# A decode kernel bound by its loads: the last query tile of four weights loads goes to the upper 64 partitions by GpSimd's queue

## The chip, the cores and the metric

The kernel runs on one core of one Trainium2 chip. The metric is device time in microseconds, the median of several executions. TensorE (PE), VectorE (DVE), ScalarE (ACT), GpSimd (POOL) and SyncE (SP) run side by side, and 16 DMA engines move data between HBM and SBUF for all of them. A transfer is issued by SyncE, ScalarE or GpSimd, each through a queue of its own. SBUF has 128 partitions.

## The reference

Two layers of attention with a cached K and V (one new token, batch 2, 32 query heads over 8 K/V heads, 32,768 cached positions, head size 128), each followed by a token-mixing MLP. All values are float32.

```python
def _A_ref(x, k_cache, v_cache, wq, wo):
    q = (lambda x, *d: x.transpose(*d))((x @ wq).reshape(B, Sq, Hq, Dh), 0, 2, 1, 3)
    k = jnp.repeat(k_cache, rep, axis=1)
    v = jnp.repeat(v_cache, rep, axis=1)
    scores = jnp.einsum("bhqd,bhkd->bhqk", q, k) * (Dh ** -0.5)
    p = _softmax(scores, axis=-1)
    o = jnp.einsum("bhqk,bhkd->bhqd", p, v)
    return (lambda x, *d: x.transpose(*d))(o, 0, 2, 1, 3).reshape(B, Sq, Hq * Dh) @ wo
...
x = x + _A_ref(_layernorm(x, axis=-1), A_k_cache, A_v_cache, A_wq, A_wo)
x = x + _B_ref(_layernorm(x, axis=-1), B_w1, B_b1, B_w2, B_b2)
x = x + _A_ref(_layernorm(x, axis=-1), A_k_cache, A_v_cache, A_wq, A_wo)
x = x + _B_ref(_layernorm(x, axis=-1), B_w1, B_b1, B_w2, B_b2)
```

K and V of all heads and both batch entries are 537 MB, and each layer reads them once.

## The kernel before

The work is cut into units: one K/V head of one batch entry in one layer, 32 units in all. A unit reads K in eight chunks of 4,096 positions and then V in eight chunks. A chunk is 128 partitions by 16 KB, 2 MB. TensorE multiplies the query of the unit with the K chunks (`k_chunk`, line 426, tile `scores`), VectorE takes the maximum and transposes, ScalarE makes the exponentials (line 466), TensorE multiplies them with the V chunks (`v_chunk`, line 581, tile `acc`), and the output projection of the unit is added to a row in PSUM (`add_row`, line 246). V of a unit runs interleaved with K of the next.

Nearly the whole of SBUF is one tile, `mem`, in cells of one chunk. Cells 0 to 8 are the ring for K and V, cells 9 to 12 (`WCELL0` and on) hold weights, and a rest of five 512-word pieces follows. Cell 8 also serves as `spot()`, a turning supply of eight 512-word scratch tiles for query rows and hidden tiles.

The order of everything is written out at build time. A list `stream` holds all K and V loads in order; the loop at the end goes through it, issues each load from SyncE's queue (`load`, line 139) and the matmuls of its chunks, and counts time in chunks. Other steps are hung on that clock by `at(time, step)`: for instance the query of a unit is made about six chunks before its K begins (`make_q`, `q_products`, line 340), and the weights come ten chunks before.

Weights (`load_weights`, line 118) come for two heads at a time: four query tiles and four output tiles of 128 rows by 2 KB for each head, so 32 KB in each of 128 partitions, 4 MB, in one load from SyncE's queue. There are four pairs of heads; one pair stays for both layers, so there are seven such loads. The query of a unit is the sum of four matmuls with `xnT`, the normalised input in columns, one for each query tile.

GpSimd makes constants at the start and the powers of the layer norms (lines 271, 685, 871); it issues no transfer.

Of the kernel before, what the change touches and what calls it, by code (L numbers as in the profile page):

```python
# [13 lines left out]
P = 128  # L14
CK = 4096
# [5 lines left out]
RING = 3  # L21
# [9 lines left out]
KEPT_Q = 4  # L31
RESIDENT = (5, 7)
TWO_HEADS = ((0, 1), (2, 3), (4, 6), RESIDENT)
FOLLOWS = {2: (2.2, -0.9, -0.8, -0.7, 3.5, -0.6, -0.5, -0.4), 5: (3.05, 0.1, 0.2, 0.3, 5.1, 3.1, 3.2, 3.3)}
PIECES = (32, 16, 8, 4, 4)
THIN = 16
QT = 4
# [7 lines left out]
def gqa_mixer_kernel(ctx: ExitStack, tc: tile.TileContext, x, kt, v, wqo, cols, out):  # L45
# [17 lines left out]
    nc = tc.nc  # L63
    B, D = out.shape
# [4 lines left out]
    R = wqo.shape[2] // (4 * D)  # L69
    DT = D // P  # L70
    FT = (cols.shape[1] - 1) // 4
# [13 lines left out]

    NP = 28 + 32 * 2
    widths = dict(x=B * DT, xn=B * DT, q=KEPT_Q * R, cols=4 * FT + 1, ident=P, one=1, half=1, selg=R * QT)
    widths |= dict(selh=R, mask=QT, others=B, oz=2 * R * B, qpads=NP, unit=2 * 16, ln=16 + 2 * FT)
    small_sb = const.tile([P, sum(widths.values())], F32, name="small_sb")
    sm, w0 = {}, 0  # L90
    for name, w in widths.items():
# [6 lines left out]
    W = wqo.shape[2] // 4  # L98
    assert CK == 2 * W
    WCELL0, WCELLS = RING * RING, 4  # L100
    heads = list(range(HKV))
    passing = [h for h in heads if h not in RESIDENT]
    home = {}
    mem = const.tile([P, (WCELL0 + WCELLS) * CK + REST * QT * DH], F32, name="mem")

    def cells(k, m=1):
        return mem[:, k * CK : (k + m) * CK]

    def wq_at(h):
        return cells(home[h])[:, :W].rearrange("p (t c) -> p t c", t=DT)  # L110

    def wo_at(h):
        return cells(home[h])[:, W:].rearrange("p (t c) -> p t c", t=R)

    def load_weights(k, cell):
        for j in range(2):
            home[TWO_HEADS[k][j]] = cell + j
        nc.sync.dma_start(cells(cell, 2), wqo[k])


    busy = [0] * 2 * (WCELL0 + WCELLS + 1)
# [73 lines left out]
    ident = sm["ident"]  # L195
# [59 lines left out]
    def first_input():  # L255

        t = spot()
        cen, sq = (t[:, k * B * DT : (k + 1) * B * DT].rearrange("p (b d) -> p b d", b=B) for k in range(2))
        m, rs = (t[:, (2 * DT + k) * B : (2 * DT + k + 1) * B] for k in range(2))
        p = misc()  # L260
        nc.tensor.matmul(p[:, : B * DT], ones, xcols.rearrange("p b d -> p (b d)"), start=True, stop=True)
        nc.vector.tensor_reduce(m, p[:, : B * DT].rearrange("p (b d) -> p b d", b=B), axis=AX.X, op=ALU.add)
        nc.vector.tensor_scalar_mul(m, m, 1.0 / D)
        for b in range(B):
            nc.vector.tensor_scalar_sub(cen[:, b, :], xcols[:, b, :], m[:, b : b + 1])
        nc.vector.tensor_mul(sq, cen, cen)
# [27 lines left out]
    xnT = sm["xn"].rearrange("p (d b) -> p d b", b=B)  # L294
# [5 lines left out]
    spots = [0]  # L300

    def spot():

        spots[0] += 1
        return cells(RING * RING - 1)[:, spots[0] % (CK // D) * D :][:, :D]

    def to_columns(key):

# [12 lines left out]
    def unit_of(n):  # L321

        return units[n]

    q_ps, q_row, q_kept = {}, {}, {}
    kept_q = [0]

    def partner(n):

        layer, b, h = unit_of(n)  # L330
        return units.index((layer, B - 1, h)) if b == 0 and (layer == 0 or h in passing) else None

    def q_products(n, *ds):

        layer, b, h = unit_of(n)
        m = 1 if partner(n) is None else B
        for d in ds:
            if d == 0:
                q_ps[n] = bcast if N1 < n <= N3 + 2 else kept[0]
            nc.tensor.matmul(  # L340
                q_ps[n][:m, :],
                xnT[:, d, b : b + m],
                wq_at(h)[:, d, :],
                start=(d == 0),
                stop=(d == DT - 1),
            )

    def make_q(n, step, place=None):

# [339 lines left out]
    ln = sm["ln"]  # L689
# [238 lines left out]
    kbeg, k_done, vbeg, v_done, vend_of, v_from, v_to, brings, starts, t = {}, {}, {}, {}, {}, {}, {}, [], [], 0  # L928
# [13 lines left out]
    def at(time, f, *a, rank=1):  # L942
        done.setdefault(time, []).append((rank, f, a))

    HC = NCH // HALVES
    opens = {two[0]: k for k, two in enumerate(TWO_HEADS)}
    mixed = {}
    for n in range(NU):
        layer, b, h = unit_of(n)
# [19 lines left out]
                assert max(v_done[n - 2, c] for c in range(HC)) <= q2  # L969
        if n and h in opens and (units[n] == (0, 0, h) or h in passing and units[n] == (1, 0, h)):  # L970
            at(kbeg[n] - (7 if n == N3 + 2 else 10), load_weights, opens[h], WCELL0 + opens[h] % 2 * 2)
        if n in (N1 + 1, N2 + 1):
            at(kend - 0.5, turn_scores, n, 0, rank=2)
            at(kend, q_products, n + 1, 0)
            at(kend, max_1, n)
            at(kend, q_products, n + 1, 1)
            at(kend, max_2, n)
            at(kend, exponentials_at_once, n, 0)
            at(kend, q_products, n + 1, 2, 3)
            t1 = kend + 2  # L980
            assert mixed[units[n - 1][:2]] == kend == kbeg[n + 1] - 2
            at(t1, turn_scores, n, 1, rank=2)
            at(t1, exponentials_at_once, n, 1, rank=2)
            at(t1 + 1, sums, n)
            assert t1 + 1 < v_done[n, HC] - 1
        else:
            t1 = max(kend + 2, ahead + (2 if urgent else 4))
            e = kend if N1 < n <= N3 else kend + 2
            at(max(kend, e - 1), max_1, n)
            at(e, max_2, n)  # L990
            t0 = max(k_done[n, HC - 1], *(v_done[n - 1, c] for c in range(HC) if n), 0)
            if n in (N2, N3):
                t0 = max(t0, kbeg[n + 1] - 3)
            at(t0, turn_scores, n, 0)
            at(e, exponentials, n, 0)
            if n == NU - 1:
                t1 = ahead
                assert t1 >= kend + 2 and vbeg[n] == ahead
            at(t1, turn_scores, n, 1)
            at(t1, exponentials, n, 1)  # L1000
# [74 lines left out]
    t = 0  # L1075
# [11 lines left out]
    assert not done, sorted(done)  # L1087


def _layout(A_x, A_k_cache, A_v_cache, A_wq, A_wo, B_w1, B_b1, B_w2, B_b2):  # L1090

    import numpy as np

    B, HKV, SK, DH = A_k_cache.shape
    D = A_x.shape[-1]
    n = SK // CK


    keys = np.arange(SK).reshape(n, CK)
    for c0, m in GROUPS:  # L1100
        keys[c0 : c0 + m] = keys[c0 : c0 + m].reshape(P, m, CK // P).transpose(1, 0, 2).reshape(m, CK)
    k = keys.reshape(n // PACK, PACK // 2, 2, NG, 32, JT // QT, QT // SUB, SUB)
# [11 lines left out]
    return {  # L1114
        "x": np.ascontiguousarray(A_x.reshape(B * (D // P), P).T),
        "kt": kt,
        "v": A_v_cache.reshape(B * HKV, SK * DH),
        "wqo": np.stack([np.concatenate([wqo[h] for h in two], axis=1) for two in TWO_HEADS]),
        "cols": np.concatenate(cols, axis=1),
    }  # L1120

# [24 lines left out]
```

## Time and profile before

| what | value |
|---|---|
| time, median of 3 (lowest to highest) | 2491.02 us (2490.99 to 2491.31) |
| the profiled execution: its own time, its span | 2490.09 us, 2488.0 us |
| moved by DMA | 1062.51 MB, mean 427 GB/s |
| TensorE, VectorE, ScalarE, GpSimd busy | 55%, 10%, 8%, 0% |
| mean granted TensorE clock | 0.772 |

Busy shares are over the whole span. A row of a stretch gives the length, then busy time and number of instructions of each engine, the granted clock, the busy share of the 16 DMA engines (counted where a packet starts) and GB/s. A row of a DMA queue gives packets, MB and the time that its packets took as a share of 16 engines over the stretch.

### The profile page before, as it was taken

The page shows a single profiled execution, that of the slowest core. Times are in us where ns is not written, and L with a number is a line of the kernel's source. Part 1 is how long each engine was busy: PE and PEld are TensorE (multiplying, and loading weights), DVE is VectorE, ACT ScalarE, POOL GpSimd, SP SyncE. Part 2 cuts the span into 40 slices and gives each one's busy share as a digit, 9 for nine tenths or more (in the row PEclk, how much of TensorE's full clock was granted, in tenths as well). Part 3 has the DMA queues.
Part 4 walks back from the last instruction along what each step waited for, and adds up shares of the span by engine and source line. Part 5 has one row for each costly group of instructions (what it writes and reads, how often), then busy time and mean ns, then how long its engine had stood idle before and what let it go on. Part 6 is the DMA issues. An engine that isn't in the chain of part 4 may idle for free.

```text
span 2488.0 us, 20543 instructions
## 1 busy us (share of the span) xinstructions
PE 1371.4 (55%) x9302; PEld 376.2 (15%) x9302; DVE 244.9 (10%) x643; ACT 187.7 (8%) x554; POOL 4.9 (0%) x17
## 2 busy tenths in 40 slices
PE   4544445544545454657677665455455465455546
PEld 1111111111111111111121121111111111111112
DVE  1000000000000000003113110000000000010002
ACT  0000000000000000002012000000000000011002
POOL 0000000000000000000000000000000000000000
PEclk8777767876777777778888887777678677777878
DMA  9999999999999999999999999999999999999996
GB/s 421 437 432 428 433 436 430 434 435 427 436 436 432 426 436 431 427 431 407 433 427 417 428 432 432 438 430 431 432 428 438 428 429 435 431 434 431 432 431 291
DMA packets 30336, 1062.51 MB, mean 427 GB/s; under 512 B 3621, under 2 KB 3625, under 8 KB 4266
## 3 DMA queue, kind: packets, MB, share of 16 engines
q1 hardware_dynamic: 29960, 1061.17, 99.1%
q8 instruction: 73, 1.20, 0.2%
q14 instruction: 13, 0.11, 0.0%
q10 hardware_dynamic: 290, 0.04, 0.0%
HBM read 1061.19 MB, written 0.00 MB: 427 GB/s over the span
## 4 chain that ended last, share of the span: by engine, by line
DMA 73%; PE 25%; DVE 1%; issue 0%; another core or an unknown queue 0%; ACT 0%; SPq 0%; POOL 0%; ACTq 0%
DMA mem<-in_v_dram 64%; PE acc L581 20%; DMA mem<-in_kt_dram 9%; PE scores L426 3%; PE small L612 0%; PE small L455 0%; PE small L449 0%; PE bcast L340 0%; ACT S L466 0%; PE small L642 0%; PE kept L246 0%; PE kept L792 0%; PE bcast L672 0%; DVE S L551 0%
## 5 line engine op out<-in xcount | busy, mean ns | idle before, releaser
L426 PE MATMUL scores<-mem,small_sb 128*32 128x512 f32 x4096 | 631.7, 736 | 605.4 <-DMA mem<-in_kt_dram 605.2
L581 PE MATMUL acc<-mem,S 128*16 128x512 f32 x4088 | 596.8, 723 | 457.1 <-DMA mem<-in_v_dram 447.7
L426 PEld LDWEIGHTS scores<-mem,small_sb 128*32 128x32 f32 x4096 | 150.0, 129 | 988.7 <-issue 903.7
L466 ACT ACTIVATE S<-S,small_sb 128x128 f32<-128x128 f32 x240 | 123.4, 517 | 2107.9 <-DVE small_sb L457 1556.9
L581 PEld LDWEIGHTS acc<-mem,S 128*16 128x16 f32 x4088 | 132.6, 109 | 810.8 <-issue 664.4
L441 DVE TENSOR_REDUCE small_sb<-scores 128x1 f32<-128x512 f32 x64 | 44.2, 691 | 819.5 <-PE scores L426 819.5
L461 DVE STREAM_TRANSPOSE S<-scores 128x512 f32<-128x512 f32 x64 | 45.5, 710 | 116.0 <-PE acc L581 116.0
L340 PE MATMUL kept<-mem,small_sb 128*2 128x512 f32 x104 | 51.1, 617 | 1.7 <-DVE small_sb L274 1.7
L466 ACT ACTIVATION_READ_ACCUMULATOR S<-S,small_sb 128x1 f32 x240 | 44.7, 186 | 0.0
L246 PE MATMUL kept<-mem,small_sb 128*1 128x512 f32 (+1 forms) x236 | 42.4, 598 | 2.6 <-ACT mem L835 2.4
L451 DVE TENSOR_REDUCE small_sb<-small 1x4 f32<-1x128 f32 x32 | 8.9, 279 | 277.7 <-PE small L449 277.7
L614 DVE RECIPROCAL small_sb<-small 128x4 f32<-128x4 f32 x32 | 5.9, 185 | 304.6 <-PE small L612 304.6
L623 DVE TENSOR_TENSOR small_sb<-small,small_sb 128x4 f32<-128x4 f32 x31 | 5.1, 164 | 295.8 <-PE small L621 295.8
L551 DVE SCALAR_TENSOR_TENSOR S<-acc,small_sb,S 128x128 f32<-128x128 f32 x93 | 32.6, 351 | 3.3
L835 ACT ACTIVATE S<-bcast,small_sb 128x512 f32<-128x512 f32 x28 | 21.5, 777 | 87.2 <-DVE small_sb L704 85.1
L366 PE MATMUL small<-small_sb,mem 2*128 2x2 f32 x112 | 15.5, 256 | 17.9 <-DVE mem L362 17.9
L549 DVE TENSOR_SCALAR S<-acc,small_sb 128x128 f32<-128x128 f32 x31 | 10.8, 350 | 147.3 <-PE acc L581 147.3
L621 PEld LDWEIGHTS small<-small_sb,S 128*128 128x128 f32 x62 | 12.7, 258 | 48.8 <-issue 41.2
L340 PE MATMUL bcast<-mem,small_sb 128*1 128x512 f32 (+1 forms) x40 | 19.4, 600 | 0.0
L366 PEld LDWEIGHTS small<-small_sb,mem 2*128 2x128 f32 x112 | 14.3, 196 | 30.5 <-DVE mem L362 27.3
L852 DVE SCALAR_TENSOR_TENSOR acc<-S,small_sb,acc 128x512 f32<-128x512 f32 x24 | 18.1, 755 | 2.5
L449 PE MATMUL small<-small_sb 128*1 128x128 f32 x64 | 16.6, 353 | 3.1 <-DVE small_sb L447 3.1
(147 smaller groups left out, 285.3 us busy)
## 6 DMA issues: line engine op xcount, KB each, us to landing
mem<-in_kt_dram SPq DMA_DIRECT2D x14, 4096.0 KB, 22.5
mem<-in_v_dram SPq DMA_DIRECT2D x11, 4096.0 KB, 29.2
mem<-in_wqo_dram SPq DMA_DIRECT2D x7, 4096.0 KB, 37.6
mem<-in_v_dram SPq DMA_DIRECT2D x13, 2048.0 KB, 21.3
mem<-in_kt_dram SPq DMA_DIRECT2D x12, 2048.0 KB, 19.3
mem<-in_kt_dram SPq DMA_DIRECT2D x24, 1024.0 KB, 8.8
mem<-in_v_dram SPq DMA_DIRECT2D x21, 1024.0 KB, 8.8
mem<-in_kt_dram SPq DMA_DIRECT2D x2, 6144.0 KB, 24.2
```

Source lines behind the costliest of these rows:

```text
L246: nc.tensor.matmul((rows if to is None else to)[32 * g : 32 * g + b + 1, :], weights if b else weights[:, 1:], row, start=to is not None, ...
L340: nc.tensor.matmul(q_ps[n][:m, :], xnT[:, d, b : b + m], wq_at(h)[:, d, :], start=(d == 0), stop=(d == DT - 1),)
L366: nc.tensor.matmul(pt[:, r * m : (r + 1) * m], q_row[n][:m, r * DH : (r + 1) * DH], ident[:m, :m], start=True, stop=True,)
L426: nc.tensor.matmul(sc_ps[n, half][32 * g : 32 * g + 32, :], q, kc[k * NG + g], start=(i == 0 and k == 0), stop=(i == PACK - 1 and k == SUB ...
L441: nc.vector.tensor_reduce(mx[n][:, half : half + 1], sc_ps[n, half], axis=AX.X, op=ALU.max)
L449: nc.tensor.matmul(pm[:1, :P], mxa, ident, start=True, stop=True)
L461: nc.vector.transpose(S[half], sc_ps[n, half])
L466: nc.scalar.activation(s[:, :, h], s[:, :, h], AF.Exp, bias=neg[n][:, h : h + 1], scale=SCALE, accum_out=lsum[n][:, half, h : h + 1],)
L551: nc.vector.scalar_tensor_tensor(t, acc[:, k * DH : (k + 1) * DH], mask[:, k : k + 1], t, op0=ALU.mult, op1=ALU.add)
L581: nc.tensor.matmul(acc[32 * g : 32 * g + R * QT, :], S[half][:, col : col + R * QT], vc[q], start=(c == v_from[n] and q < NG), stop=(c == ...
L835: nc.scalar.activation(hid[key, f], px[key], AF.Gelu_apprx_tanh, bias=shift[key][:, f : f + 1], scale=slope[key][:, f : f + 1],)
L852: nc.vector.scalar_tensor_tensor(h if f == FT - 1 else acc, h, w, acc, op0=ALU.mult, op1=ALU.add)
```

## The change

In the loads of two pairs of heads (`UPPER`, heads 2, 3 and 4, 6), once in each layer, the last of the four query tiles of each head is left out of the load from SyncE's queue, which so becomes 28 KB in each partition. The two tiles left out go as four half tiles, 64 rows each, to partitions 64 to 127, where the two halves of a tile lie side by side: in the rest of `mem` for one pair, in the upper half of cell 8 for the other (`raise_tiles`). They go by eight loads of eight rows, every fourth partition, from GpSimd's queue, 18 chunks ahead of the weights load. Ahead of each of the eight stands a load of two words to each of eight partitions of a small tile, `step`, which nothing reads. The product with the last query tile becomes two matmuls over 64 partitions each; for this the last column block of `xnT` is also copied, its lower half to partitions 64 to 127 (`raise_input`). `spot()` turns among four tiles instead of eight. The weights of those pairs are laid out to fit.

```diff
+UPPER = (1, 2)
...
     def load_weights(k, cell):
+        tiles = 2 * (DT + R - (k in UPPER))
         for j in range(2):
-            home[TWO_HEADS[k][j]] = cell + j
-        nc.sync.dma_start(cells(cell, 2), wqo[k])
+            home[TWO_HEADS[k][j]] = cell * CK + j * (tiles // 2) * D
+        of = wqo[k].rearrange("p c -> (p c)")[: P * tiles * D].rearrange("(p c) -> p c", p=P)
+        nc.sync.dma_start(mem[:, cell * CK :][:, : tiles * D], of)
+
+    lift = {UPPER[0]: 0, UPPER[1]: 1}
+    steps = [0]
+
+    def raise_tiles(k):
+        lift[k] = 1 - lift[k]
+        w0 = (WCELL0 + WCELLS) * CK if lift[k] else (WCELL0 - 1) * CK + CK // 2
+        for j in range(2):
+            raised[TWO_HEADS[k][j]] = [mem[H:, w0 + (2 * i + j) * D :][:, :D] for i in range(2)]
+        of = wqo[k].rearrange("p c -> (p c)")[-H * 4 * D :].rearrange("(i u c) -> u i c", i=2, u=H)
+        to = mem[H:, w0 : w0 + 4 * D].rearrange("u (i c) -> u i c", i=2)
+        nc.vector.memset(sm["step"], 0.0)
+        for r in range(8):
+            u = r % 4 + H // 2 * (r // 4)
+            i = steps[0] % 16
+            steps[0] += 1
+            nc.gpsimd.dma_start(sm["step"][i::16, ::2], cols[i::16, :3:2])
+            nc.gpsimd.dma_start(to[u : u + 29 : 4], of[u : u + 29 : 4])
+
+    def raise_input():
+        p = misc()
+        nc.tensor.matmul(p[H:, :B], ident[:, :H], xnT[:, DT - 1, :], start=True, stop=True)
+        nc.vector.tensor_copy(sm["up"][H:, :], p[H:, :B])
...
-        return cells(RING * RING - 1)[:, spots[0] % (CK // D) * D :][:, :D]
+        return cells(RING * RING - 1)[:, spots[0] % (CK // D // 2) * D :][:, :D]
...
+            last = d == DT - 1
+            pairs = [(xnT[:, d, b : b + m], wq_at(h, d))] if not (last and h in raised) else [
+                (x[H:, b : b + m], t) for x, t in zip((xnT[:, d, :], sm["up"]), raised[h])
+            ]
+            for i, (x, t) in enumerate(pairs):
+                nc.tensor.matmul(
+                    q_ps[n][:m, :], x, t, start=(d == 0), stop=(last and i == len(pairs) - 1)
+                )
...
             at(kbeg[n] - (7 if n == N3 + 2 else 10), load_weights, opens[h], WCELL0 + opens[h] % 2 * 2)
+            if opens[h] in UPPER:
+                at(kbeg[n] - 28, raise_tiles, opens[h])
+                if opens[h] == UPPER[0]:
+                    at(kbeg[n] - 28, raise_input)
```

GpSimd's instructions after the start-up, before the change: a constant for the padded queries, the power of the first layer norm, then those of the mixers.

```order
L218 MEMSET small_sb 128x16
L220 MEMSET small_sb 128x92
L271 TENSOR_TENSOR mem<-mem,small_sb 128x2
L685 TENSOR_TENSOR small_sb<-small_sb 128x1
L871 TENSOR_TENSOR small_sb<-small_sb 128x1
```

The same place now; `small_sb<-in_cols_dram` is a tiny load, `mem<-in_wqo_dram` one of the eight-row loads:

```order
L251 MEMSET small_sb 128x16
L253 MEMSET small_sb 128x92
L304 TENSOR_TENSOR mem<-mem,small_sb 128x2
L144 DMA small_sb<-in_cols_dram 8x2x1
L145 DMA mem<-in_wqo_dram 8x2x1024
```

The last two rows come 16 times in a row here, in two groups of eight, and 16 times again in layer 1, after the powers of the layer changes.

TensorE at the query of the fifth unit (head 2, first layer), before; `kept_85` is the PSUM tile of the query products:

```order
L426 MATMUL scores<-mem,small_sb 32x512 x15
L340 MATMUL kept_85<-mem,small_sb 2x512 [waits DMAHW7_49]
L340 MATMUL kept_85<-mem,small_sb 2x512
L426 MATMUL scores<-mem,small_sb 32x512 x8
L340 MATMUL kept_85<-mem,small_sb 2x512 x2
```

And now; the names with SW are semaphores of GpSimd's transfers:

```order
L378 MATMUL kept_85<-mem,small_sb 2x512 [waits DMAHW7_49]
L378 MATMUL kept_85<-mem,small_sb 2x512
L460 MATMUL scores<-mem,small_sb 32x512 x8
L378 MATMUL kept_85<-mem,small_sb 2x512
L378 MATMUL kept_85<-mem,small_sb 2x512 [waits DMASW5_49,DMASW7_49,DMASW3_49,DMASW1_49]
L378 MATMUL kept_85<-mem,small_sb 2x512
L460 MATMUL scores<-mem,small_sb 32x512 x8
```

The fourth product has become two, and the first of them waits for the raised tiles. SyncE's list of loads has the same order and number, four of them with 7,168 words in a partition instead of 8,192.

More of the change, by code (lines that the diff above doesn't have):

```diff
@@ L87, in gqa_mixer_kernel @@
     widths = dict(x=B * DT, xn=B * DT, q=KEPT_Q * R, cols=4 * FT + 1, ident=P, one=1, half=1, selg=R * QT)
-    widths |= dict(selh=R, mask=QT, others=B, oz=2 * R * B, qpads=NP, unit=2 * 16, ln=16 + 2 * FT)
+    widths |= dict(selh=R, mask=QT, others=B, oz=2 * R * B, qpads=NP, unit=2 * 16, ln=16 + 2 * FT, step=3, up=B)
     small_sb = const.tile([P, sum(widths.values())], F32, name="small_sb")
@@ L107, in cells, with wq_at @@
         return mem[:, k * CK : (k + m) * CK]
-    def wq_at(h):
-        return cells(home[h])[:, :W].rearrange("p (t c) -> p t c", t=DT)
+    H = P // 2
+    raised = {}
+    def wq_at(h, d):
+        return mem[:, home[h] + d * D :][:, :D]
     def wo_at(h):
-        return cells(home[h])[:, W:].rearrange("p (t c) -> p t c", t=R)
+        w = home[h] + (DT - (h in raised)) * D
+        return mem[:, w : w + W].rearrange("p (t c) -> p t c", t=R)
     def load_weights(k, cell):
+        tiles = 2 * (DT + R - (k in UPPER))
         for j in range(2):
-            home[TWO_HEADS[k][j]] = cell + j
-        nc.sync.dma_start(cells(cell, 2), wqo[k])
+            home[TWO_HEADS[k][j]] = cell * CK + j * (tiles // 2) * D
[21 more added lines that the diff above has]
+        nc.vector.tensor_copy(sm["up"][H:, :], p[H:, :B])
     busy = [0] * 2 * (WCELL0 + WCELLS + 1)
@@ L339, in q_products @@
                 q_ps[n] = bcast if N1 < n <= N3 + 2 else kept[0]
[L340 to L346, printed above, removed]
+            last = d == DT - 1
[6 more added lines that the diff above has]
+                )
     def make_q(n, step, place=None):
@@ L1087, in gqa_mixer_kernel, with _two_heads @@
     assert not done, sorted(done)
+def _two_heads(two, parted, d):
+    import numpy as np
+    if not parted:
+        return np.concatenate(two, axis=1)
+    c = np.arange((d // P - 1) * d, d // P * d)
+    main = np.concatenate([np.delete(a, c, axis=1) for a in two], axis=1)
+    top = [np.concatenate([a[u : u + P // 2, c] for a in two], axis=1) for u in (P // 2, 0)]
+    return np.concatenate([a.ravel() for a in (main, *top)]).reshape(P, -1)
 def _layout(A_x, A_k_cache, A_v_cache, A_wq, A_wo, B_w1, B_b1, B_w2, B_b2):
@@ L1117, in _layout @@
         "v": A_v_cache.reshape(B * HKV, SK * DH),
-        "wqo": np.stack([np.concatenate([wqo[h] for h in two], axis=1) for two in TWO_HEADS]),
+        "wqo": np.stack([_two_heads([wqo[h] for h in two], k in UPPER, D) for k, two in enumerate(TWO_HEADS)]),
         "cols": np.concatenate(cols, axis=1),
```

## The prediction

> **What bounds the kernel now.** I read the page first, then stretches of the span, then SyncE's issues, and last single packets of the DMA engines. On the page:
>
> ```profile
> span 2488.0 us, 20543 instructions
> PE 1371.4 (55%) x9302; PEld 376.2 (15%) x9302; DVE 244.9 (10%) x643; ACT 187.7 (8%) x554; POOL 4.9 (0%) x17
> DMA  9999999999999999999999999999999999999996
> q1 hardware_dynamic: 29960, 1061.17, 99.1%
> q8 instruction: 73, 1.20, 0.2%
> DMA 73%; PE 25%; DVE 1%; issue 0%; another core or an unknown queue 0%; ACT 0%; SPq 0%; POOL 0%; ACTq 0%
> ```
>
> TensorE is busy for 55% of the span, while SyncE's queue q1 keeps all 16 DMA engines busy for 99.1% of it and the chain that ended last is DMA for 73%. The waits say the same: the scores matmuls stand idle until a K chunk lands. And SyncE issues a load well before the engines are free for it (rows of its timeline; the landing row is that of the seven weights loads):
>
> ```profile
> PE scores L426 <- DMA mem<-in_kt_dram: 605.2, 82, 20.3
> 218.40 0.33 SPq L139 DMA_DIRECT2D mem<-in_v_dram  x1
> 218.77 0.43 SPq L118 DMA_DIRECT2D mem<-in_wqo_dram  x1
> 237.31 0.33 SPq L139 DMA_DIRECT2D mem<-in_kt_dram  x1
> DMA to landing us min/median/max: 12.3/37.6/37.8
> ```
>
> The weights issued at 218.77 take the median 37.6 us to land, and the next K load is issued 19 us after them, so there is always work queued. What counts is therefore not the mean of the 16 engines but the engine that is last. Here are stretches of the span: a long one inside layer 0, the first change of layer, and the last microseconds of the loads. The last two numbers of a row are the busy share of the 16 engines and GB/s.
>
> ```profile
> 240.00:560.00 320.00, 162.82 (x1120) 44.49 (x1120) 22.45 (x64) 16.32 (x61) 0.00 (x0) 0.75 1.00 433
> 1120.00:1200.00 80.00, 58.87 (x390) 14.83 (x390) 25.67 (x50) 14.11 (x19) 1.08 (x2) 0.86 1.00 412
> 2462.00:2464.00 2.00, 2.00 (x24) 0.65 (x20) 0.00 (x0) 0.00 (x0) 0.00 (x0) 1.00 1.00 424
> 2466.00:2467.00 1.00, 0.57 (x8) 0.25 (x12) 0.00 (x0) 0.00 (x0) 0.00 (x0) 1.00 0.92 367
> 2467.00:2468.00 1.00, 1.00 (x16) 0.12 (x4) 0.00 (x0) 0.00 (x0) 0.00 (x0) 1.00 0.59 240
> 2468.00:2469.00 1.00, 0.44 (x8) 0.10 (x8) 0.00 (x0) 0.00 (x0) 0.00 (x0) 1.00 0.48 193
> 2469.00:2470.00 1.00, 0.95 (x8) 0.03 (x6) 0.00 (x0) 0.00 (x0) 0.00 (x0) 1.00 0.48 188
> 2470.00:2471.00 1.00, 0.80 (x24) 0.43 (x24) 0.91 (x3) 0.00 (x0) 0.00 (x0) 1.00 0.33 123
> 2471.00:2472.00 1.00, 0.76 (x18) 0.31 (x10) 0.56 (x3) 0.00 (x0) 0.00 (x0) 1.00 0.08 16
> ```
>
> The share falls in two steps: from 1.00 to one half at about 2467.3, and from one half to nothing at about 2470.8. So eight engines (I call them the early half) finish some 3.5 us ahead of the other eight (the late half), though every load in q1 gives all 16 the same bytes. The late half sets the end. Who makes it late the rows do not label; the 73 instruction fetches of queue q8 are the likely cause, but nothing below needs that.
>
> **The change, part by part.** *The bytes.* Each of the four weights loads shrinks by one eighth: 2 of 16 tiles of 128 rows x 2 KB, 524,288 bytes, or 32,768 for each engine. The same bytes come back through GpSimd's queue in eight transfers of 8 rows. If each of these falls on the same eight engines, those carry 65,536 bytes and the others none. Over four loads one half gains 131,072 bytes per engine and the other half loses as much. At 433 GB/s an engine moves 27.06 GB/s, so this is 4.84 us, plus for one half and minus for the other. The total is unchanged. The sign of the change hangs on which half gets them.
>
> *Which half.* The trace before has one load or store of few rows in mid-stream: ScalarE's store of one row of the output, 2 KB, issued at 2311.48. A row of 10 ns holds one packet: GB/s times 10 ns is its size. The K load of those packets was issued at 2309.68 and took 25.9 us to land.
>
> ```profile
> 2309.68 0.33 SPq L139 DMA_DIRECT2D mem<-in_kt_dram  x1
> 2311.48 0.51 ACTq L882 DMA_DIRECT2D out_dram<-mem  x1
> mem<-in_kt_dram SPq DMA_DIRECT2D x1, 25.9
> 2313.79:2313.80 0.01, 0.00 (x0) 0.00 (x0) 0.00 (x0) 0.01 (x1) 0.00 (x0) 1.00 15.12 6554
> 2316.21:2316.22 0.01, 0.00 (x0) 0.00 (x0) 0.00 (x0) 0.00 (x0) 0.00 (x0) 0.50 0.53 205
> 2316.29:2316.30 0.01, 0.01 (x4) 0.01 (x8) 0.00 (x0) 0.00 (x0) 0.00 (x0) 0.50 15.11 6554
> 2328.38:2328.39 0.01, 0.00 (x0) 0.00 (x0) 0.00 (x0) 0.00 (x0) 0.00 (x0) 1.00 15.14 6554
> 2330.80:2330.81 0.01, 0.00 (x0) 0.00 (x0) 0.00 (x0) 0.00 (x0) 0.00 (x0) 0.50 15.17 6554
> ```
>
> A 64 KB packet starts at 2313.79, the 2 KB one 2.42 us later at 2316.21, the next 64 KB one 0.08 us after that, and the same engine goes on every 2.42 us to 2328.38 and 2330.80. The packet at 2330.80 opens the next load, so this engine was through with the K load 4.8 us before it had landed everywhere (2309.68 + 25.9 = 2335.6). The store's engine belongs to the early half. A transfer that needs few engines thus began with one of the early half. The tiny load stands first in each pair; if GpSimd's queue begins where that store did and deals on in order, the tiny ones get the early half and the tiles get the late half. That is my likeliest case, and it is an inference: no GpSimd load is in this trace. [...]
>
> *The packets' own cost.* GpSimd's queue, which had no transfer, gets a tiny load and a tile load in turn. There are now 64 transfers: 32 tiny ones of 8 x 2 words, 32 of 8 x 2 pieces of 4 KB. Nearest rows for what a packet of another queue costs, first the start-up stretch from 3 to 13 us, then the stretch of 55.8 to 57.1 us with one instruction fetch:
>
> ```profile
> q10 hardware_dynamic: 144, 0.00, 0.8%
> q8 instruction: 1, 0.02, 5.3%
> ```
>
> The first gives 0.8% of 160 us over 144 packets, 8.9 ns each. The second gives 5.3% of 20.8 us, 1.10 us for 16,384 bytes that take 0.61 us at the full rate: a surplus of 0.49 us. I take 8.9 ns, since the added packets are words and plain rows like the first. If each of the 64 completes on every engine: 64 x 8.9 ns = 0.57 us on all, and 32 x 2 x 8.9 ns = 0.57 us on the half with the tiny ones. The upper bound is a fetch's surplus at each of 32 visits, 15.7 us.
>
> *TensorE, and who waits.* For each pair of heads the last query product becomes two matmuls, the first of which waits on four of GpSimd's transfers, with a scores chunk behind it.
>
> ```profile
> L340 PE MATMUL kept<-mem,small_sb x104: 592/592/1057, 17.3 to 2034.9; 128*2 128x512 f32 x104
> 1152.84 0.54 POOL L685 TENSOR_TENSOR small_sb<-small_sb 128x1 f32<-128x1 f32 x1 [1136.03 <-DVE small_sb L702]
> 2229.82 0.54 POOL L685 TENSOR_TENSOR small_sb<-small_sb 128x1 f32<-128x1 f32 x1 [869.45 <-DVE small_sb L702]
> ```
>
> Eight such matmuls more make 8 x 0.592 = 4.7 us, hidden in the 605 us that scores wait for K; without that cover 4.7 us. The wait costs nothing: the tiles are issued 28 chunks ahead and the product runs 5 ahead; a chunk is 2 MB, 4.84 us, so 111 us lie between. On GpSimd only the powers stand behind the transfers, at 1152.84 and 2229.82; the raises come 18 chunks, 87 us, before the weights load, the first at about 132 us, each layer's two well ahead of its powers, and nobody waits. The four memsets and two copies on VectorE (10% busy), two matmuls with the identity, and half as many spare tiles in `spot` (ScalarE's hidden tiles then wait for a reader four tiles back, each a chunk apart) are nothing beside it. SyncE keeps its order of loads; its K load at the change of layer waits for tiles landed long before.
>
> *Sum, likeliest case.* The late half gets 4.84 + 0.57 = 5.4 us more, nothing hides it, and the compute behind the last load is as before: 2490.09 us for the profiled execution becomes 2495.5. The median of the runs stands 0.93 us above it, so I forecast 2491.02 + 5.4 = 2496.4 us.
>
> **The rivals.** *The tiles fall on the early half.* Then the late half gets -4.84 + 0.57 + 0.57 = -3.7 us: 2487.3. The early half must have room: at the end its lead is 3.5 us, and it grows by 5.4 us of work, which taken alone would make it the last at 2467.3 + 5.4 = 2472.7, 1.9 us after today's end at 2470.8 (2492.9). But it also stands waiting earlier: at the change of layer only 412 of 433 GB/s flow, 3.9 us of 80 for all or 7.8 for one half, in part because of that stage's small rows. That slack is there to be used, so I hold -3.7. For it: two of the four loads lie on each side of the change of layer, so the extra work meets slack twice. Against it: the store's engine.
>
> *No steering: the rows spread evenly over all 16.* Then only the packets cost, 0.57 + 0.28 = 0.9 us: 2491.9. The change would not do what it says. Against it: the number of rows is half the number of engines. [...]
>
> *The visits cost like fetches.* Each of the 32 visits stalls an engine by 0.49 us: 15.7 us on both halves, with tiles on the late one 2491.0 + 15.7 + 5.4 = 2512.1. It decides from a surplus of about 0.1 us per visit on. For it: the fetch row; against it: q10's row.
>
> **How the numbers follow.** Likeliest case 0.50, early half 0.22, even spread 0.20, dear visits 0.08. The range reaches from 2486.2 (early half with packets that cost nothing, 2491.02 - 4.84) to 2498.0 (likeliest case with 0.05 us more per visit, 1.6 us); the dear visits lie outside. The likeliest case alone spans 2495.4 (half of the packet cost and 0.7 us absorbed by fetch gaps) to 2498.0. A measurement of this kernel can tell about 0.2% from no change, 5.0 us: bounds 2486.0 and 2496.0. The likeliest case lies just over the upper one, about 0.62 of it beyond: 0.31, with the dear visits 0.39. Faster than 2486.0 needs more than all the bytes: 0.04. The rest, 0.57, is the same.
>
> **What would show it.** In the new profile the last microseconds tell: if I am right, the share falls to one half earlier before the end, with about 3.5 + 10 us between the steps less what the early half loses by waiting, the second step at about 2476. If the tiles went to the early half, the two steps draw together and the end comes near 2467; with an even spread they stay 3.5 us apart. GpSimd's queue should show 512 packets of 4 KB at about the full rate; a mean far over 0.16 us would mean dear visits. A wait of TensorE at the split product would show the raise comes too late, which I rule out.

## The result and the profile after

The changed kernel takes 2500.81 us (median of 6 runs, 2498.49 to 2502.39) against 2491.16 us (6 runs, 2490.04 to 2491.74): 1.0039 times as long, 95% interval 1.0026 to 1.0052. I had forecast 2496.4 us in a range of 2486.2 to 2498.0. The sign was right and the size too small: 9.65 us instead of 5.4.

The page of the changed kernel:

```profile
span 2497.9 us, 20681 instructions
DMA  9999999999999999999999999999999999999996
q1 hardware_dynamic: 29960, 1059.08, 98.7%
q0 software_dynamic: 2560, 2.11, 0.3%
DMA 73%; PE 24%; issue 1%; DVE 1%; another core or an unknown queue 0%; ACT 0%; SPq 0%; POOL 0%; ACTq 0%; POOLq 0%
```

The kernel is bound as before, by DMA for 73% of the chain. GpSimd's queue q0 carries 2560 packets: the 512 of 4 KB that I counted, and 2048 small ones of some 9 ns each, where I had counted 1536 (1024 completions and 512 words of the tiny loads). In the trace's single packets a 4 KB one takes 0.16 us, as forecast.

When does the delay come? These are rows of TensorE's timeline where it waits for a K or V chunk: the start of the first matmul on it, its busy time, and in brackets the idle time before it. The same six chunks, one behind each raise and two, the third and the fourth, on either side of the change of layer, first in the kernel before:

```profile
295.37 3.44 PE L581 MATMUL acc<-mem,S 128*16 128x512 f32 x16 [3.73 <-DMA mem<-in_v_dram]
596.89 6.30 PE L426 MATMUL scores<-mem,small_sb 128*32 128x512 f32 x32 [19.73 <-DMA mem<-in_kt_dram]
1045.09 1.92 PE L426 MATMUL scores<-mem,small_sb 128*32 128x512 f32 x16 [1.16 <-DMA mem<-in_kt_dram]
1527.75 5.09 PE L426 MATMUL scores<-mem,small_sb 128*32 128x512 f32 x32 [3.25 <-DMA mem<-in_kt_dram]
1781.03 6.44 PE L426 MATMUL scores<-mem,small_sb 128*32 128x512 f32 x32 [19.59 <-DMA mem<-in_kt_dram]
2140.61 3.64 PE L426 MATMUL scores<-mem,small_sb 128*32 128x512 f32 x16 [10.01 <-DMA mem<-in_kt_dram]
```

and then in the changed one (line 460 is the old 426, 615 the old 581):

```profile
297.19 3.62 PE L615 MATMUL acc<-mem,S 128*16 128x512 f32 x16 [3.33 <-DMA mem<-in_v_dram]
600.49 2.79 PE L460 MATMUL scores<-mem,small_sb 128*32 128x512 f32 x12 [19.07 <-DMA mem<-in_kt_dram]
1048.94 1.50 PE L460 MATMUL scores<-mem,small_sb 128*32 128x512 f32 x12 [1.18 <-DMA mem<-in_kt_dram]
1533.66 1.94 PE L460 MATMUL scores<-mem,small_sb 128*32 128x512 f32 x8 [4.49 <-DMA mem<-in_kt_dram]
1788.58 1.94 PE L460 MATMUL scores<-mem,small_sb 128*32 128x512 f32 x8 [19.18 <-DMA mem<-in_kt_dram]
2150.32 2.74 PE L460 MATMUL scores<-mem,small_sb 128*32 128x512 f32 x9 [9.50 <-DMA mem<-in_kt_dram]
```

The matmuls start 1.8, 3.6, 3.9, 5.9, 7.6 and 9.7 us later: 1.6 to 2.2 us for each raise, and 2.1 us more from 3.9 to 5.9, where there is no raise but the change of layer. The last microseconds, in stretches of 2 us (the last two numbers are DMA share and GB/s):

```profile
2472.00:2474.00 2.00, 2.00 (x24) 0.59 (x20) 0.00 (x0) 0.00 (x0) 0.00 (x0) 1.00 1.00 418
2474.00:2476.00 2.00, 0.98 (x12) 0.06 (x4) 0.00 (x0) 0.00 (x0) 0.00 (x0) 1.00 0.84 335
2476.00:2478.00 2.00, 1.80 (x16) 0.36 (x16) 0.00 (x0) 0.00 (x0) 0.00 (x0) 1.00 0.59 226
2478.00:2480.00 2.00, 1.23 (x16) 0.20 (x16) 0.22 (x1) 0.00 (x0) 0.00 (x0) 1.00 0.32 123
2480.00:2482.00 2.00, 1.67 (x34) 0.77 (x34) 1.46 (x5) 0.00 (x0) 0.00 (x0) 1.00 0.02 8
```

The share still falls in two steps, at about 2475.7 and 2479.5, so the halves end some 4 us apart, hardly more than the 3.5 before. Yet eight engines were relieved of 4.84 us and the other eight got as much. At first it shows: the trace has the landing of each load on each of the 16 engines, and at about 295 us, behind the first raise, the middle of the late half lands 4.1 us behind the middle of the early one, where it was 1.5 in the kernel before; the bytes of one raise are 2 x 1.21 us. At about 470 us the two are 2.2 and 2.1 us, so the relief is gone. How the early half loses it, the stretch behind the second raise shows. SyncE's issues there, and 20 us of the engines, of the changed kernel and then of the one before:

```profile
563.71 0.33 SPq L172 DMA_DIRECT2D mem<-in_kt_dram  x1
581.49 0.33 SPq L172 DMA_DIRECT2D mem<-in_v_dram  x1
614.93 0.33 SPq L172 DMA_DIRECT2D mem<-in_kt_dram  x1
600.00:620.00 20.00, 15.57 (x86) 4.45 (x90) 1.57 (x5) 0.00 (x0) 0.00 (x0) 0.84 0.95 401
```

```profile
610.11 0.33 SPq L139 DMA_DIRECT2D mem<-in_kt_dram  x1
600.00:620.00 20.00, 14.85 (x93) 4.50 (x89) 1.67 (x6) 0.00 (x0) 0.00 (x0) 0.77 1.01 437
```

The K load at 614.93 waits for TensorE to be through with an older chunk, and that chunk was ready only once the late half had brought it (600.49). By then the early half has emptied its queue: the share is 0.95 instead of 1.01 and 401 GB/s flow instead of 437. An engine that was ahead by more than the queued work stood still here, and its lead was not saved for later. The load is issued 4.8 us later than before (610.11), though the older chunk came only 3.6 us later: two query products more, of 0.59 us each, stand between the scores and the release of the buffer.

In the single packets no more than 10 of the 16 engines have one in flight from 614.25 to 615.75 us, where in the kernel before all 16 do. The same happens at 449.0 us (9 of 16), and there the packets are slow as well when the engines start again: at 449.1 us six of 64 KB begin within 0.2 us and take 3.0 to 3.7 us instead of 2.42. The stretch around them, in the changed kernel and then in the one before:

```profile
445.00:455.00 10.00, 5.56 (x35) 1.83 (x37) 1.57 (x5) 0.00 (x0) 0.00 (x0) 0.88 0.95 380
```

```profile
445.00:455.00 10.00, 4.36 (x24) 1.65 (x25) 0.79 (x4) 0.00 (x0) 0.00 (x0) 0.68 0.98 426
```

### The profile page after: what moved, and what is told of

Read it like the earlier page. It is cut to its first block, busy times and chain, and to the rows that moved or that the text cites. A ratio compares the mean times of both kernels' runs of the same rounds, so it can differ in the third digit from the quotient of the medians.

```text
span 2497.9 us, 20681 instructions
## 1 busy us (share of the span) xinstructions
PE 1382.2 (55%) x9322; PEld 373.4 (15%) x9322; DVE 245.3 (10%) x649; ACT 188.1 (8%) x554; POOL 41.1 (2%) x81
## 3 DMA queue, kind: packets, MB, share of 16 engines
q0 software_dynamic: 2560, 2.11, 0.3%
## 4 chain that ended last, share of the span: by engine, by line
DMA 73%; PE 24%; issue 1%; DVE 1%; another core or an unknown queue 0%; ACT 0%; SPq 0%; POOL 0%; ACTq 0%; POOLq 0%
DMA mem<-in_v_dram 65%; PE acc L615 20%; DMA mem<-in_kt_dram 8%; PE scores L460 3%; PE bcast L378 0%; PE small L646 0%; PE small L489 0%; PE small L483 0%; ACT mem L848 0%; PE kept L279 0%; PE small L676 0%; PE bcast L706 0%; DVE S L585 0%; ACT S L500 0%
## 5 line engine op out<-in xcount | busy, mean ns | idle before, releaser
L378 PE MATMUL kept<-mem,small_sb 128*2 128x512 f32 (+1 forms) x120 | 58.9, 614 | 1.7 <-DVE small_sb L307 1.7
L144 POOL DMA_DIRECT2D small_sb<-in_cols_dram x32 | 18.1, 565 | 892.4 <-DVE small_sb L151 452.0
L145 POOL DMA_DIRECT2D mem<-in_wqo_dram x32 | 18.1, 565 | 189.2 <-issue 189.1
```

What stands on the lines that cost most here:

```text
L144: nc.gpsimd.dma_start(sm["step"][i::16, ::2], cols[i::16, :3:2])
L145: nc.gpsimd.dma_start(to[u : u + 29 : 4], of[u : u + 29 : 4])
L378: nc.tensor.matmul(q_ps[n][:m, :], x, t, start=(d == 0), stop=(last and i == len(pairs) - 1))
```

## The experiments

The theories at first: A, the forecast with dearer packets (the tiles on the late half, some 0.5 us of packet cost for each raise); B, transfers of GpSimd's queue stop the engines by themselves; C, partitions 64 to 127 get too much. `e1` swaps the two loads of a pair, `e2` drops the tiny ones, `e3` adds only tiny loads to the kernel before, `e4` raises by one 64-row load from SyncE's queue.

**e1: tile load first**

```diff
-            nc.gpsimd.dma_start(sm["step"][i::16, ::2], cols[i::16, :3:2])
             nc.gpsimd.dma_start(to[u : u + 29 : 4], of[u : u + 29 : 4])
+            nc.gpsimd.dma_start(sm["step"][i::16, ::2], cols[i::16, :3:2])
```

> The order of each pair of GpSimd's loads is turned: the tile load first, the tiny one behind it. Theory A (the eight-row loads fall on the late eight DMA engines, 4.84 us of bytes, plus about 0.5 us of packet cost per group of 16 transfers): the tiles move to the early half, the late half is relieved, 2488 to 2490 us, 1 to 3 us below the kernel before. Theory B (GpSimd's transfers as such stop the DMA engines for about 2 us per group, whoever gets them): as with the change, about 2500 us. Theory C (what counts is the destination: partitions 64 to 127 get more bytes than their side of SBUF takes in): as with the change, about 2500 us.

Measured 2515.83 us, 1.0099 times before (1.0086 to 1.0113). All three theories missed. Stretches of the second and the fourth raise, of the changed kernel first and of e1 second:

```profile
485.00:565.00 80.00, 40.65 (x272) 10.76 (x272) 5.24 (x15) 3.94 (x16) 7.82 (x14) 0.72 1.00 431
1860.00:1940.00 80.00, 43.54 (x290) 11.72 (x290) 5.96 (x17) 4.29 (x16) 6.73 (x12) 0.79 1.01 431
```

```profile
485.00:565.00 80.00, 35.55 (x252) 9.37 (x248) 5.28 (x16) 4.29 (x16) 7.33 (x13) 0.74 1.01 411
1860.00:1940.00 80.00, 42.76 (x290) 11.53 (x282) 5.96 (x17) 4.29 (x16) 6.76 (x12) 0.78 1.00 409
```

The engines are as busy (share 1.00) but move 20 GB/s less. In the single packets all 16 engines are slower: while a tile load is in flight the median 64 KB packet takes 2.5 to 2.75 us, mostly 2.6 to 2.7, between two of them 2.42 to 2.44. In the changed kernel it stays at 2.42 to 2.43 throughout.

**e2: no tiny loads**

```diff
-        nc.vector.memset(sm["step"], 0.0)
...
-            nc.gpsimd.dma_start(sm["step"][i::16, ::2], cols[i::16, :3:2])
```

> The 32 tiny loads and their memset are left out, the 32 eight-row loads stay. Theory A: successive loads alternate between the two halves, so both get the bytes they had before, and only half the packet cost stays: 2492 to 2493 us. Theory B: half the transfers, half the loss, about 2496 us. Theory C: the bytes still go to partitions 64 to 127: 2498 to 2500 us.

Measured 2502.07 us (1.0049, 1.0035 to 1.0063), again outside all three. Without the memset to wait for, its first raise is under way before 25 us. In the single packets every second tile load slows the 64 KB packets to 2.59 us and the ones between leave them at 2.43: I read this as loads that take two groups of eight engines in turn, one of which is slow for them.

**e3: only tiny loads**

```diff
+                nc.gpsimd.dma_start(sm["step"][i::16, 0:3:2], cols[i::16, :3:2])
+                nc.gpsimd.dma_start(sm["step"][i::16, 3:6:2], cols[i::16, :3:2])
...
+            if opens[h] in (1, 2):
+                at(kbeg[n] - 28, tiny_loads)
```

> The kernel before with its full weights loads, and 64 tiny loads by GpSimd's queue at the four places (two tiny ones for each pair of the change). Nothing else is moved. Theory A: the packet cost alone, 2493 to 2494 us. Theory B: nearly the whole loss, 2499 to 2501 us. Theory C: no loss, 2491 to 2492 us.

Measured 2550.95 us (1.024), far above all three. The waits of e3 show why, and that it does not answer its question:

```profile
PE small L459 <- DMA small_sb<-in_cols_dram: 72.0, 4, 18.3
```

With this layout of the small tile the scheduler made four transposes of the running maximum wait for all sixteen tiny loads, 18 us each, and TensorE stood. The changed kernel has no such wait. `e9` repeats it without the flaw.

**e4: one 64-row load from SyncE's queue**

```diff
-        for r in range(8):
...
-            nc.gpsimd.dma_start(to[u : u + 29 : 4], of[u : u + 29 : 4])
+        nc.sync.dma_start(to, of)
```

> The raised tiles go by one load of 64 rows from SyncE's queue for each pair of heads in place of GpSimd's sixteen transfers. Theory A: 64 rows spread over all 16 engines, each with the bytes it had before: 2491 to 2492 us. Theory B: no GpSimd transfer, no loss: 2491 us. Theory C: the destination is as in the change: 2496 to 2500 us.

Measured 2511.38 us (1.0082, 1.0068 to 1.0095), once more outside all three. The stretch of the first raise, in the kernel before and then in e4:

```profile
140.00:180.00 40.00, 19.92 (x144) 5.04 (x140) 3.95 (x10) 2.11 (x8) 0.00 (x0) 0.79 1.01 438
```

```profile
140.00:180.00 40.00, 16.49 (x116) 4.19 (x112) 3.21 (x9) 2.11 (x8) 0.00 (x0) 0.70 1.02 400
```

438 GB/s become 400: slow again, without GpSimd, where theory B saw no loss: B falls. The same target leaves the 64 KB packets of the changed kernel at 2.42 us, so C falls in its plain form too. What fits e1, e2 and e4 is theory P, an inference: the first group of eight engines serves partitions 0 to 63 in whole-width loads, the second 64 to 127, and a tile load that crosses to the other group's partitions slows everything. The next runs test it.

**e6 and e7: the tiles on partitions 0 to 63** (in e6 the tile load first, in e7 the tiny one, as in the change)

```diff
-        to = mem[H:, w0 : w0 + 4 * D].rearrange("u (i c) -> u i c", i=2)
+        to = mem[:H, w0 : w0 + 4 * D].rearrange("u (i c) -> u i c", i=2)
...
-        nc.tensor.matmul(p[H:, :B], ident[:, :H], xnT[:, DT - 1, :], start=True, stop=True)
+        nc.tensor.matmul(p[:H, :B], ident[:, H:], xnT[:, DT - 1, :], start=True, stop=True)
```

> As e1 (tile load first in each pair, tiny load behind it), but the two 64-row tiles lie on partitions 0 to 63 instead of 64 to 127 (and the small matmul with the identity moves the input's upper half down). Theory P (each group of eight engines has its own 64 partitions in the whole-width loads, and a tile load that crosses to the other group's partitions slows the 64 KB packets of all 16 engines from 2.42 to about 2.6 us while it lasts): the first group's tiles no longer cross; packets stay at 2.42 to 2.43 us, and the time falls from e1's 2516 to 2488 to 2493. Theory G (the first group is slow for these packets, wherever they go): 2514 to 2518 as in e1. Theory H (any work that lands on the half that is behind costs it, and nothing else matters; e1's loss has another cause, the order of the two loads): as e1.

> As the change (tiny load first, tile load second), but the two 64-row tiles lie on partitions 0 to 63. Theory P (crossing to the other group's partitions slows all packets): now the second group's tiles cross, 64 KB packets go to about 2.6 us during the raises, and the time is 2512 to 2520, like e1. Theory G (the first group is the slow one): 2498 to 2503, like the change. Theory H (the order tile first is what costs): like the change.

Measured: e6 2498.78 us (1.0028, 1.0017 to 1.0039), e7 2518.65 us (1.0109, 1.0096 to 1.0123), in P's range. The same two stretches, e6 and then e7:

```profile
485.00:565.00 80.00, 38.68 (x272) 10.34 (x272) 5.27 (x15) 5.34 (x22) 7.32 (x13) 0.77 1.00 432
1860.00:1940.00 80.00, 46.21 (x290) 12.14 (x290) 5.96 (x17) 4.31 (x16) 5.61 (x10) 0.76 1.01 430
```

```profile
485.00:565.00 80.00, 36.24 (x256) 9.87 (x252) 5.29 (x16) 4.29 (x16) 7.30 (x13) 0.74 1.01 410
1860.00:1940.00 80.00, 45.27 (x290) 12.09 (x290) 5.96 (x17) 4.29 (x16) 7.31 (x13) 0.75 1.00 407
```

Turning the target round turns the slow order round. P holds, and the change does not cross. Between kernels that put the same bytes on the same group, crossing costs 17.1 us (e1 less e6) and 17.8 us (e7 less the change). But e6 itself missed P's 2488 to 2493: with the tiles on the early half, uncrossed, the kernel is slower than before, too.

**e8: no GpSimd, 8-row loads from SyncE's queue to partitions 0 to 63**

```diff
-            nc.gpsimd.dma_start(to[u : u + 29 : 4], of[u : u + 29 : 4])
+        nc.sync.dma_start(to[u : u + 29 : 4], of[u : u + 29 : 4])
```

> No load from GpSimd's queue: the tiles on partitions 0 to 63, by eight loads of 8 rows per raise from SyncE's queue, two chunks apart. If a transfer of 16 pieces from SyncE's queue takes the same eight engines each time, and these are the early half with its own partitions (theory P with steering): packets stay at 2.42 us, the late half is 4.6 us lighter: 2486 to 2491. If the 16 pieces go to all 16 engines, half of them cross: 64 KB packets slow down during each load, 2496 to 2506. [...]

Measured 2497.66 us (1.0025, 1.0016 to 1.0034), above the first case and in the range of the second. Yet the 64 KB packets stayed at 2.42 us while the tile loads ran (all but a dozen, at about 1881 us), so by theory P nothing crossed, and it is not the second case: the eight engines are those of the lower partitions, the early half as in e6. With no tiny loads and no GpSimd, putting the bytes there still costs 6 us. In the kernel before, the landings of the loads on the two halves are 1.5 us apart where the first raise comes; 2 x 1.21 us more for one half than for the other would turn them round and make the early half the late one. That is argued: the trace does not say which half an engine belongs to.

**e9: only tiny loads, without e3's wait**

```diff
+            for i in (2 * r, 2 * r + 1):
+                nc.gpsimd.dma_start(sm["step"][i::16, ::2], cols[i::16, :3:2])
```

> The kernel before, with the 64 tiny loads from GpSimd's queue and nothing moved, as e3, but with the columns of the tiny tile laid out as in the change, so that no matmul of TensorE waits for them (in e3 four transposes of the running maximum waited 72 us in all for all sixteen tiny loads). If the tiny loads cost only their packets (2048 of 9 ns, 18 us over 16 engines): 2492 to 2493. If each group of loads from GpSimd's queue stops the engines for about 2 us, as theory B had it: 2499 to 2501. If e3's 60 us were the tiny loads' own cost: 2550.

Measured 2493.43 us, 1.0008 (0.9999 to 1.0017): 2.0 us, just above the first case, with an interval from nothing to 4 us. That rules out B once more.

**e10: only one of the two raises of a layer, as in e8**

```diff
-UPPER = (1, 2)
+UPPER = (2,)
```

> As e8 (tiles on partitions 0 to 63, 8-row loads from SyncE's queue, which take the early half), but only the weights load with the larger lead is split, one per layer instead of two: before it the early half is 2.8 us ahead in layer 0 and 3.4 us in layer 1, so 2.9 us more imbalance brings the halves level instead of putting the early half behind. Theory L (what a raise puts on one half counts only so far as it makes or leaves that half the last one; what it takes from the other is lost again when that half runs dry): the lead falls to about zero after each raise, and the time is 2489.5 to 2493. Theory M (each raise costs about 1.6 us whichever half it is put on, from the packets and restarts themselves): 2494 to 2496, half of e8's loss.

Measured 2494.81 us (1.0015, 1.0006 to 1.0024): in theory M's range, not in L's. In its landings the raise of layer 0 cost nothing (a V load at 1061 us lands 0.1 us later than before, and the lead falls from 4.9 to about 3 us), as L has it; some 2.5 us came at the change of layer and the rest behind the raise of layer 1. Inconclusive: one raise less costs half as much, for a reason that the run does not isolate.

**e11 and e12: each group its own rows** (rows 0 to 63 and 64 to 127 in turn, where they lay before; e12 swaps the turns)

```diff
-            nc.gpsimd.dma_start(sm["step"][i::16, ::2], cols[i::16, :3:2])
-            nc.gpsimd.dma_start(to[u : u + 29 : 4], of[u : u + 29 : 4])
+            for v in (u, H + u):
+                nc.gpsimd.dma_start(to[v : v + 29 : 4], of[v : v + 29 : 4])
```

> The same four loads are shrunk and the same bytes go through GpSimd's queue in transfers of 8 rows, but nothing is steered or raised: of each pair of transfers, the first (first group of eight engines) brings 8 rows of the tile to partitions 0 to 63, the second (second group) 8 rows to 64 to 127, where they lay before; the query product stays one matmul. No tiny loads. Theory P (a group's own partitions): 64 KB packets stay at 2.42 to 2.43 us. Theory L (only an imbalance costs): 2491.5 to 2494, the price of 512 packets of 4 KB and of their completions. If GpSimd's transfers cost something by themselves beyond that: 2496 to 2500.

> As e11, with the two transfers of each pair in the other order, so that the first group brings rows to partitions 64 to 127 and the second to 0 to 63: the same bytes on every engine, every transfer crossed. Theory P: 64 KB packets of all engines at about 2.6 us while the transfers run, 2505 to 2520. If only the balance of the halves matters: as e11.

Measured 2504.57 us (1.0053, 1.004 to 1.0066) and 2505.18 us (1.0055, 1.0042 to 1.0069), e11 above all of its ranges. They don't show what they were meant to: loads of 8 rows in single pieces did not take the groups in turn as those of two pieces each did. In the single packets the loads to partitions 0 to 63 leave the 64 KB packets at 2.43 us and those to 64 to 127 bring them to 2.6 or 2.7, in e11 the second of each pair and in e12 the first, so by P all went through one group. That is the plainest sign that the target decides, with the same queue and the same size of load in one run, though no run here gives an engine's number. The even spread is left untried.

**e13: first raise of a layer on the late half, second on the early one**

```diff
+    def side(k):
+        return slice(H, P) if k == UPPER[0] else slice(0, H)
...
+            for t, s in pair if k == UPPER[0] else pair[::-1]:
+                nc.gpsimd.dma_start(t, s)
```

> The change with its first raise of each layer as it is (tiny load first, tiles on partitions 64 to 127, so on the late half) and its second turned round (tile load first, tiles on partitions 0 to 63, so on the early half, and none of them crosses). The same bytes, packets and transfers as in the change, but over a layer both halves carry the same. Theory L (what a raise adds to the half that is behind counts, and the other half's relief is lost when it runs dry; the tiny loads cost 2.0 us as in e9): the lead goes up by 2.5 us at the first raise and comes back at the second, the early half hardly runs dry after it, and the time is 2493 to 2496. Theory M (each raise costs 1.7 us or more whichever half it is put on): 2498 to 2501, as the change and as e6.

Measured 2495.25 us (1.0014, 1.0004 to 1.0023), in L's range and outside M's. The same bytes, packets and transfers as the change, none crossed, and it is 3.66 us above its runs of before, where the change is 9.65 above its own: 6.0 us are gone. Its rows at the second, the fifth and the sixth of the six chunks, and the stretch in which the change ran dry:

```profile
598.93 4.50 PE L467 MATMUL scores<-mem,small_sb 128*32 128x512 f32 x20 [17.47 <-DMA mem<-in_kt_dram]
1785.26 5.22 PE L467 MATMUL scores<-mem,small_sb 128*32 128x512 f32 x32 [18.61 <-DMA mem<-in_kt_dram]
2144.54 3.64 PE L467 MATMUL scores<-mem,small_sb 128*32 128x512 f32 x16 [9.39 <-DMA mem<-in_kt_dram]
600.00:620.00 20.00, 15.77 (x92) 4.17 (x86) 1.57 (x5) 0.00 (x0) 0.00 (x0) 0.84 1.00 430
```

Delays of 2.0, 4.2 and 3.9 us instead of 3.6, 7.6 and 9.7: each raise on the early half adds next to nothing after one on the late half, and the engines no longer run dry there (share 1.00). Not all that is left comes from the loads. In the profiled execution, which took 2496.35 us, TensorE starts on the last chunk at 2476.54 us, 5.1 us later than before (2471.47), but the work behind it takes 1.5 us longer, at a granted clock of 0.83 in its first 10 us instead of 1.00 (e13, then the kernel before):

```profile
2476.00:2486.00 10.00, 8.12 (x70) 4.57 (x71) 5.46 (x16) 2.79 (x4) 0.54 (x1) 0.83 0.00 1
```

```profile
2472.00:2482.00 10.00, 8.36 (x112) 5.27 (x114) 7.89 (x21) 5.28 (x6) 0.54 (x1) 1.00 0.00 0
```

No kernel tried beats the one before.

## Why the prediction was wrong

- *What bounds it, and the two halves:* right. The share falls in two steps in both profiles, and the late half sets the end.
- *Which half gets the tiles:* right. The chunks are later behind each raise, the landings of the halves are 4.1 us apart instead of 1.5 behind the first one, and e1, e2, e6 and e7 fit two groups taken in turn from the first on, with the tiles of the change on the second. The two steps at the end, which were to show it, could not: they are hardly further apart than before, as the prediction had it for an even spread, because the early half lost its relief by waiting.
- *The bytes, 4.84 us:* about right as a term. Taking the imbalance away (e13) gave 6.0 us back, a difference of medians that is good to some 4 us. That includes what the restarts cost where the early half ran dry, which the prediction named only as something that would narrow the steps.
- *The packets' own cost, 0.57 us, as all that the sum had beside the bytes:* this is the step that failed. What is left when the imbalance is gone is 3.7 us (e13, 1.0014, from 1.0 to 5.7 us by its interval). The small packets by themselves measured 2.0 us (e9): 2048 of 9 ns, spread evenly, are 1.15 us for each engine, where I put 0.57 us on the late half, and the interval of e9, nothing to 4 us, leaves open whether they cost more than their own time. In the rows of the changed kernel the four raises add 7.4 us, where their bytes are 4.84: 0.6 us for each raise beside the bytes. Another 2.1 us come at the change of layer (3.9 to 5.9 us), for which the sum had nothing. The same two chunks lose 0.8 us there in e13 (2.3 to 3.1) and in e9 (1.2 to 2.0). From 1365 to 1375 us the changed kernel moves 388 GB/s at a share of 0.96, the one before 404 at 0.99; what holds the loads up there is not isolated. Fewer scratch tiles do not show there: ScalarE makes twelve hidden tiles just before in 10.23 us in both. Two things more stand in the trace, neither tested alone: the packets of 4 KB, and the split products, which at 600 us held the issue of a K load back by 1.2 us, when only the early half was out of work:

```profile
L378 PE MATMUL kept<-mem,small_sb 64*2 64x512 f32 x32 | 15.0, 588 | 0.0
```

  Of these 32 matmuls half are additional, 16 of 588 ns or 9.4 us, not 4.7: I counted eight. They overlap in part, and the busy time of the query products grows by 7.8 us (51.1 to 58.9). They don't wait themselves (0.0), as forecast.
- *"Its slack is there to be used", the early half as a rival at 2487.3:* refuted by e8 (2497.66) and e6 (2498.78). With two raises in a layer the kernel loses whichever half they are put on, and the relieved half does not keep what it gains. With one (e10) the first raise cost nothing, but the kernel still lost 3.3 us.
- *Even spread, 2491.9:* not reached by any run; e11 was to show it and did not. That loads of eight rows spread over all 16 engines does not fit e6 and e7, where standing ahead of or behind the tiny loads decided between 432 and 410 GB/s over the second raise.
- *Dear visits:* not in the change, whose 64 KB packets stay at 2.42 to 2.43 us. They exist for crossing loads, and cost there 17 to 18 us; I had no such mechanism among the rivals.
- *The range:* its upper end was the likeliest case and 0.05 us for each of 32 visits. It held no bound for losses beside the bytes of the size that e9 and e13 show.

## What to carry to other kernels

When all DMA engines are full, look at the halves, not at the mean: here the half that got more bytes was late at once (4.1 us between the halves behind the first raise instead of 1.5), while the relieved half ran dry as soon as its lead exceeded the queued work (9 or 10 of 16 engines had a packet in flight at 449 and at 615 us). Which half of the partitions a load of few rows goes to counts as well: in e1 the 64 KB packets of all 16 engines took mostly 2.6 to 2.7 us instead of 2.42, and e1 and e7 took 17 to 18 us longer than e6 and the change, the same loads with the target turned round. By theory P they should go through the engines that write those partitions anyway. And price what is added beside the bytes, small packets, instructions and the next change of stage, as a term of its own, with an upper bound as wide as the main term: here 3.7 of 9.65 us were left when the imbalance was gone.

## What was not expected of the hardware

- In e1 the loads of 8 rows, which by theory P cross to the other half's partitions, slowed the 64 KB packets of all 16 engines, not only of eight, from 2.42 to 2.6 us and more: 411 GB/s over the second raise, where the change moved 431.
- Loads of 8 rows of two pieces each from GpSimd's queue slowed the 64 KB packets at every second load (e2: 2.59 us, 2.43 between), as if they took two groups of engines in turn. Loads of 8 rows of one piece slowed them when they went to partitions 64 to 127 (2.6 or 2.7 us) and not when they went to 0 to 63 (2.43), whichever came first (e11, e12), as if all went through one group. Why is open.
- With the engines full (share 0.99 from 165 to 250 us in the changed kernel), GpSimd got a load out only every 2 to 10 us, mostly 5 to 9, after the first two of a raise. From its timeline there:

```profile
163.67 0.57 POOL L145 DMA_DIRECT2D mem<-in_wqo_dram  x1
170.16 0.58 POOL L144 DMA_DIRECT2D small_sb<-in_cols_dram  x1 [5.92 <-issue]
177.56 0.56 POOL L145 DMA_DIRECT2D mem<-in_wqo_dram  x1 [6.83 <-issue]
182.44 0.55 POOL L144 DMA_DIRECT2D small_sb<-in_cols_dram  x1 [4.32 <-issue]
```

  A raise so lasted some 90 us, near the 111 us by which the tiles are issued ahead.
